# Loading two weight matrices with GpSimd's casting transfers, in a linear-attention and highway kernel

## The chip, the core and the metric

The kernel runs on one core of a Trainium2 chip. The metric is the device time of one execution in microseconds (us). Beside it stands a profile of one execution: its span runs from the first to the last instruction, and what the time has beyond the span lies around it. The engines are called PE (TensorE, matmuls and turning blocks), DVE (VectorE), ACT (ScalarE), POOL (GpSimd) and SP (SyncE, which here only issues transfers).

## The reference: what is computed

```python
q, k, v: (8, 8, 576, 64) fp32        # batch, heads, sequence, head size
q_s = softmax(q, axis=-1)            # over the 64 of a head
k_s = softmax(k, axis=2)             # over the sequence
kv  = einsum('bhsd,bhse->bhde', k_s, v)
att = einsum('bhsd,bhde->bhse', q_s, kv)
x   = att.transpose(0, 2, 1, 3).reshape(4608, 512)
H   = maximum(x @ w_h, 0)            # w_h, w_t: 512 x 512 fp32
T   = sigmoid(x @ w_t + b_t)
out = T * H + (1 - T) * x            # 4608 x 512 fp32
```

## The kernel before, in words

Every load, computation and store is a small function, and the string `ORDER` (lines 16 to 62) is a list of 683 steps, such as `mt_5_0`, that are issued one after the other. The order of the list is the order on each engine's queue and on each queue of transfers; an engine works through its own steps strictly in this order, and waits are put in where a step needs another's result or buffer. A letter behind a colon chooses the engine: `:A` is ACT, `:D` DVE, `:P` POOL, and `:F` takes a whole batch in one instruction. No planner runs when the kernel is built; the list is all there is.

The work is done batch by batch (8 batches) and in 36 tiles of 128 output rows. Nine tiles belong to two batches: four to each, and one that holds rows of both. The steps of a batch `b` are:

- `q_b_*`, `k_b_*`, `v_b_*`: loads, on SP's queue, of fp32 data. Batches 0 and 1 are loaded in pieces. A new transfer on SP waits until the eighth before it has landed, and until its buffer is free.
- `ek`, `eq`: exponentials on ACT, to fp16. `vc`: the cast of v to fp16 (POOL without a letter, or ACT, or DVE).
- `kv_b_*`: PE's products of exp(k) and v (72 small matmuls, or 36 for a half in batches 0 and 1). `kr`, `kn`: DVE divides by the sums and writes the small matrix `kvb`.
- `qt_b_g`: PE turns blocks of exp(q); `qc_b_g` copies them from PSUM to SBUF (DVE, or ACT with `:A`).

The steps of a tile `i` are:

- `xu_i`: PE multiplies turned q with `kvb`; `rs` and `x`: DVE divides by the row sums and writes x in fp16.
- `xt_i`: PE turns x into the PSUM tile `turned`; `xe_i` copies it out as `xT` (ACT, or DVE with `:D`).
- `bw_i`: the bias goes into the gate's PSUM tile, by a PE matmul or by a copy on ACT (`:A`). `mt_i`: PE multiplies `xT` with `w16["t"]`, four matmuls of 128x512. `mh_i`: the same with `w16["h"]`.
- `th_i`: tanh of half the gate on ACT. `dd_i`: DVE forms d = max(-x/2, ...) from x and the `mh` result. `uu_i`: (tanh + 1) times d, on DVE, or with `:P` as two instructions on POOL. `oo_i`: POOL adds x. `st_i`: the store, on SP's queue.

The weights are needed in fp16, and `w_h` in the form half of (w_h minus identity), so that one `max` and one product give the result. Before the change this takes four kinds of steps. `w_t_c` and `w_h_c` (line 208; c is 0 or 2, two blocks of 128 rows each) load fp32 weights, 512 KB a step, on SP's queue into a buffer of the pool for outputs (`o32`). `wtc_c` (line 217) casts w_t to fp16, here on POOL. `whd_c` (line 224) subtracts the identity from one 128x128 block in fp32, on POOL. `whc_c` (line 228) halves and casts w_h, on ACT.

Setup is part of the list as well. `setuppool` (line 148) lets POOL fill the tile `blank` with zeros and make two identity matrices; `setupdve` clears tiles on DVE. `fill_n` (line 165) issues n matmuls of `blank` that compute nothing that is used: they write into `turned`, and keep PE busy while it would wait. `bp` and `bc` spread the bias over all rows.

Of the kernel before, what the change touches and what calls it, by code (L numbers as in the profile page):

```python
# [22 lines left out]
xe_0_1 dd_3 xt_2_0 mh_0_1 mt_0_1 th_1_0 xe_2_0:D dd_0 vc_1_2:A kv_1_1 uu_1_0 oo_1_0 eq_1_0 mt_0_0 th_0_0 ek_1_0 ek_1_1
kr_1_1 bw_3 qt_1_0 vc_1_1:A kn_1_1 qc_1_0 mt_3_0 xu_5_1 uu_0_0 mh_2_0 th_3_0 bw_2 rs_5_1 x_5_1 dd_2 xu_4_1 kv_1_0
kr_1_0 eq_1_1 rs_4_1 xt_5_1 mt_2_0 th_2_0 kn_1_0 bw_5 xe_5_1:D x_4_1 xu_5_0 mt_5_1 qt_1_1 eq_1_2 rs_5_0 x_5_0 xt_5_0
xu_4_0 bw_4:A uu_3_0:P oo_3_0 xe_5_0:D mh_5_1 rs_4_0 x_4_0 mh_5_0 xt_4_1 qc_1_1:A xt_4_0 xe_4_1:D dd_5 eq_2_0 xe_4_0:D
v_4_0 mt_5_0 th_5_0 xu_6_0 qt_1_2 rs_6_0 qc_1_2 oo_0_0 mt_4_1 mh_4_1 mh_4_0 uu_2_0:P x_6_0 mt_4_0 eq_2_1 xt_6_0 xu_8_0
uu_5_0 bw_6:A xe_6_0:D qt_2_0 rs_8_0 x_8_0 mh_6_0 oo_5_0 th_4_0 xt_8_0 dd_4 uu_4_0 xu_7_0 mt_6_0 ek_2_0:F rs_7_0
vc_2_2:A bw_8 xe_8_0:D mt_8_0 x_7_0 th_6_0 xt_7_0 th_8_0 oo_2_0 vc_2_0 kv_2_0 oo_4_0 qc_2_0 q_4_0 bw_7:A qt_2_1
qc_2_1:A dd_6 uu_6_0:P oo_6_0 eq_3_0:F xe_7_0:D kr_2_0 kn_2_0 mh_8_0 xu_9_0 rs_9_0 x_9_0 mt_7_0 th_7_0 bw_9 dd_8  # L30
uu_8_0:P qt_2_2 qc_2_2:A xu_10_0 bw_10:A xt_9_0 xe_9_0:D rs_10_0 x_10_0 ek_3_0 mh_7_0 dd_7 ek_3_2 mh_9_0 xu_12_0 k_4_0
xt_10_0 k_5_0 rs_12_0 qt_3_0 xe_10_0:D x_12_0 mt_9_0 th_9_0 uu_7_0:P q_4_9 dd_9 xu_11_0 qc_3_0 vc_3_2:A xt_12_0
mt_10_0 rs_11_0 mh_10_0 x_11_0 v_5_0 q_5_0 vc_3_0 st_1_1 q_5_9 uu_9_0 dd_10 oo_7_0 kv_3_0 qt_3_1 th_10_0 oo_8_0 st_1_0
xe_12_0 bw_12:A mh_12_0 kr_3_0 qc_3_1:A kn_3_0 xu_14_0 rs_14_0 x_14_0 bw_11:A xt_11_0 xe_11_0 mt_12_0 th_12_0 qt_3_2
v_6_0 xt_14_0 oo_9_0 k_6_0 xu_13_0 q_6_0 xe_14_0 mh_11_0 dd_12 qc_3_2 mt_11_0 rs_13_0 eq_4_0:F th_11_0 uu_12_0
uu_10_0:P x_13_0 dd_11 xu_15_0 rs_15_0 vc_4_0 mh_14_0 x_15_0 st_5_1 dd_14 qt_4_0 oo_10_0 vc_4_2 xu_16_0 rs_16_0 x_16_0
xt_13_0 xe_13_0:D oo_12_0 bw_14:A bw_13:A ek_4_0:F st_3_0 mt_14_0 th_14_0 xu_17_0 rs_17_0 bw_15:A x_17_0 qc_4_0
xt_15_0 mt_13_0 kv_4_0 xe_15_0:D kr_4_0 uu_11_0:P oo_11_0 th_13_0 qt_4_1 uu_14_0:P st_3_1 mh_13_0 vc_5_2 xt_16_0
kn_4_0 mh_15_0 xe_16_0:D vc_5_0 xu_18_0 ek_5_0:F dd_13 xt_17_0 qc_4_1:A uu_13_0 xe_17_0:D dd_15 rs_18_0 oo_14_0
bw_16:A mt_15_0 mh_16_0 x_18_0 th_15_0 uu_15_0:P mt_16_0 dd_16 mh_17_0 oo_13_0 bw_17:A th_16_0 oo_15_0 kv_5_0 uu_16_0  # L40
kr_5_0 kn_5_0 oo_16_0 eq_4_2 dd_17 qt_4_2 xt_18_0 eq_5_0 mt_17_0 st_5_0 xe_18_0 xu_20_0 rs_20_0 mh_18_0 qc_4_2:A
bw_18:A q_7_0 th_17_0 mt_18_0 eq_5_1 bw_20:A uu_17_0:P x_20_0 xt_20_0 dd_18 vc_6_2 xe_20_0:D xu_21_0 th_18_0 rs_21_0
st_7_0 v_7_0 qt_5_1 qc_5_1:A mt_20_0 x_21_0 xt_21_0 uu_18_0 eq_5_2 xu_19_0 xe_21_0:D qt_5_0 rs_19_0 x_19_0 st_7_1
mh_20_0 qc_5_0 bw_21:A st_10_1 vc_6_0 mt_21_0 th_20_0 dd_20 ek_6_0:F xu_22_0 bw_19:A rs_22_0 x_22_0 qt_5_2 th_21_0
qc_5_2:A eq_6_0 mh_21_0 bw_22:A xt_19_0 xe_19_0:D kv_6_0 dd_21 kr_6_0 kn_6_0 xt_22_0 uu_20_0:P mh_19_0 mt_19_0
xe_22_0:D dd_19 oo_17_0 xu_23_0 rs_23_0 oo_20_0 oo_18_0 mt_22_0 eq_6_1 qt_6_0 th_19_0 x_23_0 xu_24_0 uu_19_0 th_22_0
xt_23_0 xe_23_0:D k_7_0 mh_22_0 rs_24_0 bw_23:A x_24_0 mt_23_0 qc_6_0 xu_25_0 rs_25_0 x_25_0 st_10_0 uu_21_0:P oo_19_0
xt_24_0 xe_24_0:D oo_21_0 mh_23_0 dd_22 uu_22_0:P xu_26_0 xt_25_0 oo_22_0 bw_24:A eq_7_0 mt_24_0 th_23_0 rs_26_0
x_26_0 qt_6_1 xe_25_0 vc_7_2 qd_7_0 xt_26_0 xu_27_0 vc_7_0 mh_24_0 dd_23 uu_23_0 rs_27_0 eq_7_1 q_7_9 qd_7_1 st_17_0
mh_25_0 x_27_0 qc_6_1:A bw_25:A xu_29_0 th_24_0 xe_26_0 dd_24 uu_24_0 mt_25_0 bw_26:A ek_7_0:F rs_29_0 x_29_0 th_25_0  # L50
oo_23_0 mh_26_0 dd_25 xt_27_0 xu_28_0 rs_28_0 xe_27_0:D x_28_0 mt_26_0 bw_27:A st_8_0 xt_29_0 xe_29_0:D eq_7_2 q_6_9
oo_24_0 mh_27_0 kv_7_0 dd_26 uu_25_0:P oo_25_0 th_26_0 xt_28_0 kr_7_0 mt_27_0 kn_7_0 mh_29_0 xe_28_0 dd_27 xu_31_0
st_14_1 bw_28:A mt_28_0 th_27_0 st_12_0 bw_29:A mt_29_0 dd_29 th_28_0 eq_6_2 rs_31_0 x_31_0 st_25_0 xu_30_0 xt_31_0
th_29_0 xe_31_0 qt_6_2 bw_31:A uu_26_0:P oo_26_0 rs_30_0 x_30_0 mh_28_0 st_12_1 uu_27_0:P st_21_0 st_14_0 qc_6_2:A
xt_30_0 xe_30_0 xu_33_0 st_16_1 oo_27_0 st_26_0 uu_29_0 oo_29_0 dd_28 st_19_0 uu_28_0:P rs_33_0 x_33_0 bw_30:A st_23_0
mh_31_0 dd_31 mt_31_0 xt_33_0 oo_28_0 xu_32_0 rs_32_0 xe_33_0:D th_31_0 mt_30_0 mh_30_0 x_32_0 qt_7_2 uu_31_0 xu_34_0
dd_30 mh_33_0 oo_31_0 bw_33:A rs_34_0 xt_32_0 x_34_0 th_30_0 xe_32_0:D qc_7_2:A uu_30_0 mt_33_0 st_28_0 st_31_0
mh_32_0 dd_33 th_33_0 uu_33_0 xu_35_0 bw_32:A rs_35_0 oo_33_0 xt_34_0 mt_32_0 bw_34:A xe_34_0:D mh_34_0 st_33_0 x_35_0
xt_35_0 mt_34_0 dd_32 th_32_0 bw_35_1 oo_30_0 st_16_0 st_30_0 uu_32_0 xe_35_0 oo_32_0 mh_35_0 th_34_0 bw_35_0 mt_35_0
th_35_0 mt_35_1 dd_34 uu_34_0 oo_34_0 dd_35 uu_35_0 st_32_0 th_35_1 uu_35_1 st_34_0 oo_35_0 st_35_0 oo_35_1:D  # L60
st_35_1:A
"""


# [1 line left out]
def kernel(  # L66
# [148 lines left out]


    def wt_cast(e, c):
        if e == "D":
            nc.vector.tensor_scalar_mul(w16["t"][:, c:c + 2], T[f"wt{c}"], 1.0)
        else:  # L220
            copy = nc.gpsimd.tensor_copy if e == "P" else nc.scalar.copy
            copy(w16["t"][:, c:c + 2], T[f"wt{c}"])

    def wh_less_identity(e, c):
        block = T[f"wh{c // 2 * 2}"][:, c % 2, c // 2 * 2 * P + c % 2:c // 2 * 2 * P + 2 * P:2]
        (nc.gpsimd if e == "P" else nc.vector).tensor_sub(block, block, idf)
# [307 lines left out]
```

## Time and profile before

| what | value |
|---|---|
| median of 3 runs | 118.77 us (118.72 to 118.85) |
| the profiled execution: its own time | 118.69 us |
| its span | 116.9 us |
| mean granted PE clock | 0.995 |
| bytes moved | 40.58 MB, of which 30.41 MB read from and 9.44 MB written to HBM |

A row of the timeline has the start and the busy time in us, the engine, the line of the code, the operation, its output and input, a count, and in brackets how long the engine sat idle before it and what ended that wait. PE's matmuls overlap, so the time of a row is longer than the distance from one to the next. Issuing a transfer is not counted as busy time.

### The profile page before, as it was taken

Reading aid. Unit: us, or ns where it says so; the run is one execution under the profiler, and the core shown is the slowest. Engines: PE = TensorE matmul, PEld = TensorE weight load, DVE = VectorE, ACT = ScalarE, POOL = GpSimd, SP = SyncE. Lnnn points to the kernel's source line nnn. Section 1 sums busy time; section 2 is a strip of 40 time slices with the busy share of each in tenths; the row PEclk is TensorE's granted clock in tenths of the full one; section 3 lists DMA queues with packets and bytes.
Section 4 is the critical chain, followed back from the end, with each engine's and each line's share of the span. In section 5 each row is a group of like instructions: output and inputs, shape, how many; then the busy total and the mean of one; then the engine's idle time right before and its main releaser. Section 6 shows DMA issues by size and latency. Waiting matters only on the chain.

```text
span 116.9 us, 3424 instructions
## 1 busy us (share of the span) xinstructions
PE 109.5 (94%) x1351; PEld 61.6 (53%) x1351; DVE 93.3 (80%) x222; ACT 90.0 (77%) x132; POOL 89.1 (76%) x99
## 2 busy tenths in 40 slices
...
GB/s 42 399 392 377 408 398 385 375 377 379 393 391 397 383 391 393 358 375 387 357 376 360 387 392 363 390 381 383 399 398 217 302 204 270 397 404 115 315 295 179
DMA packets 24195, 40.58 MB, mean 347 GB/s; under 512 B 5362, under 2 KB 11762, under 8 KB 24180
## 3 DMA queue, kind: packets, MB, share of 16 engines
...
q10 hardware_dynamic: 148, 0.14, 0.4%
...
HBM read 30.41 MB, written 9.44 MB: 341 GB/s over the span
## 4 chain that ended last, share of the span: by engine, by line
PE 67%; POOL 15%; issue 6%; DVE 5%; DMA 3%; SPq 1%; POOLq 0%; DVEq 0%
PE tps L411 18%; PE gps L419 16%; PE turned L167 9%; POOL o L471 7%; PE xu L361 6%; PE turned L384 5%; PE kv L269 5%; PE qps L324 4%; POOL u L451 4%; DMA out_dram<-o 3%; POOL g L450 2%; PE qps L319 2%; POOL v L259 2%; DVE x L376 2%; PE tps L401 1%
## 5 line engine op out<-in xcount | busy, mean ns | idle before, releaser
L471 POOL TENSOR_TENSOR o<-u,x 128x512 f32<-128x512 f16 (+1 forms) x36 | 40.6, 1143 | 1.6 <-DVE u L453 0.7
L411 PE MATMUL tps<-w16t,xT 128*128 128x512 f16 (+1 forms) x148 | 37.3, 373 | 0.0
L419 PE MATMUL gps<-w16h,xT 128*128 128x512 f16 x144 | 36.8, 379 | 0.5 <-DVE xT L391 0.5
L376 DVE TENSOR_TENSOR x<-xu,rs 128x512 f16<-128x512 f32 (+1 forms) x39 | 25.2, 649 | 2.4
L259 POOL CAST v<-v 128x1152 f16<-128x1152 f32 (+1 forms) x14 | 14.0, 1010 | 14.7 <-DMA v<-in_v_dram 13.7
L439 DVE SCALAR_TENSOR_TENSOR d<-x,gps 128x512 f16<-128x512 f16 x36 | 24.5, 680 | 0.3
L451 POOL TENSOR_TENSOR u<-g,d 128x512 f16<-128x512 f16 x17 | 19.7, 1158 | 1.7 <-DVE rs L370 0.4
L253 ACT ACTIVATE ek<-k 128x576 f16<-128x576 f32 (+2 forms) x15 | 17.9, 1225 | 3.0 <-DMA k<-in_k_dram 3.0
L419 PEld LDWEIGHTS <-xT 128*128 128x128 f16 x144 | 13.0, 98 | 12.3 <-DVE xT L391 1.8
L399 ACT COPY tps<-ball 128x512 f32<-128x512 f32 x28 | 16.6, 597 | 3.5 <-DVE u L453 3.2
L411 PEld LDWEIGHTS <-xT 128*128 128x128 f16 x148 | 13.2, 98 | 10.6 <-DVE xT L391 0.4
L361 PE MATMUL xu<-kvb,eq 128*128 128x130 f16 (+1 forms) x160 | 14.8, 224 | 0.2 <-DVE kvb L287 0.2
L384 PE MATMUL turned<-idh,x 128*128 128x128 f16 x144 | 14.2, 220 | 0.5 <-DVE x L376 0.5
L391 DVE COPY xT<-turned 128x512 f16<-128x512 f16 (+1 forms) x28 | 10.9, 391 | 4.2 <-PE turned L384 3.0
L435 ACT ACTIVATE tps<-tps 128x512 f32<-128x512 f32 (+1 forms) x20 | 11.2, 559 | 3.6 <-PE tps L411 3.3
L453 DVE SCALAR_TENSOR_TENSOR u<-tps,d 128x512 f16<-128x512 f32 (+1 forms) x19 | 12.7, 671 | 1.4 <-ACT tps L435 0.6
L361 PEld LDWEIGHTS <-eq 128*128 128x128 f16 (+1 forms) x160 | 10.0, 100 | 7.3 <-DVE x L376 2.5
L167 PE MATMUL turned<-blank 128*128 128x512 f16 x40 | 12.4, 458 | 1.5 <-POOL blank L149 1.3
L384 PEld LDWEIGHTS <-x 128*128 128x128 f16 x144 | 9.8, 98 | 6.0 <-DVE x L376 2.1
L307 ACT ACTIVATE qe<-q 128x1024 f16<-128x1024 f32 (+3 forms) x9 | 9.4, 1052 | 4.1 <-DMA q<-in_q_dram 4.1
L450 POOL TENSOR_SCALAR g<-th 128x512 f16<-128x512 f16 x17 | 10.6, 621 | 0.9 <-ACT th L433 0.9
L433 ACT ACTIVATE th<-tps 128x512 f16<-128x512 f32 x17 | 10.0, 594 | 0.9 <-PE tps L411 0.9
...
## 6 DMA issues: line engine op xcount, KB each, us to landing
...
v<-in_v_dram SPq DMA_DIRECT2D x6, 1152.0 KB, 12.0
...
```

Source lines behind the costliest of these rows:

```text
L167: nc.tensor.matmul(spare, blank[:, 0:P], blank, start=True, stop=True, skip_group_check=True)
L253: nc.scalar.activation(t[:, :, c:c + n].rearrange("p j c d -> p c j d"), T[f"k32{b}"][:, c:c + n].rearrange("p c (j d) -> p c j d", j=NJ), ...
L259: copy(v16[b % NV][:, c:c + n, :, 0:D], T[f"v32{b}"][:, c:c + n].rearrange("p c (j d) -> p c j d", j=NJ))
L361: nc.tensor.matmul(dst, turned_q(b, jp, n), kvb[b % NKV][:, hh, kk], start=True, stop=True, skip_group_check=True)
L376: nc.vector.tensor_mul(t[:, k0:k1], sums(i, k)[:, :, :, 0:64], T[f"rs{i}_{k}"][:, 0:k1 - k0].unsqueeze(3).to_broadcast([P, k1 - k0, 4, D]))
L384: nc.tensor.matmul(t[:, n], T[f"x{i}"][:, n0 + n % 2:n0 + 2 * P:2], idh, is_transpose=True, start=True, stop=True, skip_group_check=True)
L399: nc.scalar.copy(t[:, cs], ball[:, cs])
L411: nc.tensor.matmul(T[gate(i, k)][:, cs], T[f"xT{i}"][:, n], w16["t"][:, n, cs], start=False, stop=(n == parts[-1] and not first), skip_gro ...
L419: nc.tensor.matmul(t, T[f"xT{i}"][:, n], w16["h"][:, n], start=(first and n == parts[0]), stop=(n == parts[-1] and not (first and len(part ...
L439: nc.vector.scalar_tensor_tensor(t, T[f"x{i}"], -0.5, T[f"gps{i}"], op0=ALU.mult, op1=ALU.max)
L451: nc.gpsimd.tensor_mul(t, g, T[f"d{i}"])
L471: eng.tensor_add(t[:, cs], T[f"u{i}_{h}"][:, cs], T[f"x{i}"][:, cs])
```

## The change

The two weight matrices are loaded by POOL's queue instead of SP's. Such a transfer writes fp16 straight into `w16`, while it reads fp32 from HBM. The cast of w_t is then an empty step. The identity is subtracted and the half applied in place, in fp16. The weights no longer pass through the output buffers.

```diff
     def load_w(e, w, c):
         src = dict(t=moe_w_t, h=moe_w_h)[w]
-        T[f"w{w}{c}"] = op.tile([P, 2, DM], FP32, tag="o32", name=f"w32{w}_{c}")
-        nc.sync.dma_start(T[f"w{w}{c}"], src.rearrange("(c p r) n -> c p r n", p=P, r=2)[c // 2])
+        nc.gpsimd.dma_start(w16[w][:, c:c + 2], src.rearrange("(c p r) n -> c p r n", p=P, r=2)[c // 2])
...
     def wt_cast(e, c):
-        if e == "D":
-            nc.vector.tensor_scalar_mul(w16["t"][:, c:c + 2], T[f"wt{c}"], 1.0)
-        else:
-            copy = nc.gpsimd.tensor_copy if e == "P" else nc.scalar.copy
-            copy(w16["t"][:, c:c + 2], T[f"wt{c}"])
+        return
 
     def wh_less_identity(e, c):
-        block = T[f"wh{c // 2 * 2}"][:, c % 2, c // 2 * 2 * P + c % 2:c // 2 * 2 * P + 2 * P:2]
-        (nc.gpsimd if e == "P" else nc.vector).tensor_sub(block, block, idf)
+        block = w16["h"][:, c, c // 2 * 2 * P + c % 2:c // 2 * 2 * P + 2 * P:2]
+        (nc.gpsimd if e == "P" else nc.vector).tensor_sub(block, block, idh)
 
     def wh_cast(e, c):
         if e == "D":
-            nc.vector.tensor_scalar_mul(w16["h"][:, c:c + 2], T[f"wh{c}"], 0.5)
-        else:
-            nc.scalar.mul(w16["h"][:, c:c + 2], T[f"wh{c}"], 0.5)
+            nc.vector.tensor_scalar_mul(w16["h"][:, c:c + 2], w16["h"][:, c:c + 2], 0.5)
+        else:
+            nc.scalar.mul(w16["h"][:, c:c + 2], w16["h"][:, c:c + 2], 0.5)
```

The whole list of steps is also new. Its beginning, before and after:

```diff
-b_0 q_0_0 v_0_1 setupdve k_0_0 b_32 eq_0_0 bsplit setuppool fill_5 fill_8 bp v_0_0 bc qt_0_0 ek_0_1 v_0_3 ek_0_0 k_0_2
-v_0_2 vc_0_3:A bw_1 vc_0_0 ek_0_2 vc_0_2 q_0_4 vc_0_1:D ek_0_3 bw_0 w_h_0 fill_8 qc_0_0 whd_1:P kv_0_0 eq_0_1 w_h_2
-w_t_2 kr_0_0 whd_0:P whd_2:P w_t_0 k_1_2 v_1_2 q_1_0 k_1_0 v_1_0 fill_5 q_1_4 kn_0_0 q_2_0 k_2_0 eq_0_2 xu_0_0 v_2_0
-q_3_0 rs_0_0 whc_0:A x_0_0 k_3_0 fill_4 v_3_0 kv_0_1 fill_3 kr_0_1 kn_0_1 xu_0_1 rs_0_1 xu_1_0 rs_1_0 qt_0_1 x_1_0
-fill_6 whd_3:P qc_0_1 xt_1_0 xu_3_0 qt_0_2 qc_0_2:A xe_1_0:D fill_1 rs_3_0 x_3_0 x_0_1 xt_3_0 xu_2_0 rs_2_0 x_2_0
-wtc_2:P whc_2:A mh_1_0 wtc_0:P vc_1_3 ek_1_3 ek_1_2 vc_1_0 xe_3_0:D mh_3_0 dd_1 xt_0_1 xt_0_0 mt_1_0 xe_0_0:D mh_0_0
+w_t_2 setupdve setuppool fill_8 q_0_0 v_0_2 k_0_0 fill_6 b_32 b_0 bsplit bp eq_0_0 bc qt_0_0 ek_0_0 fill_8 k_0_2
+ek_0_3 bw_3 v_0_1 v_0_0 wtc_0 v_0_3 vc_0_2:D vc_0_3:D bw_1 fill_3 ek_0_1 q_0_4 qc_0_0 w_h_0 vc_0_1 fill_8 w_t_0
+vc_0_0:A kv_0_0 ek_0_2 kv_0_1 w_h_2 whd_2:P k_1_2 kr_0_0 fill_8 eq_0_1 qt_0_1 kr_0_1 v_1_2 eq_0_2 kn_0_0 kn_0_1 xu_1_0
+xu_0_0 q_1_0 whd_0 rs_1_0 x_1_0 xu_0_1 fill_5 qc_0_1:A rs_0_0 xu_3_0 x_0_0 rs_3_0 x_3_0 xt_1_0 xe_1_0 fill_5 ek_1_2
+whd_3 whd_1:P xt_3_0 mt_1_0 xe_3_0:D xt_0_0 rs_0_1 whc_2:D xu_2_0 xe_0_0 k_1_0 x_0_1 v_1_0 whc_0:D vc_1_3 rs_2_0 x_2_0
+q_1_4 qt_0_2 mt_3_0 qc_0_2 th_3_0 vc_1_2 th_1_0 mh_3_0 xt_0_1 xe_0_1:D dd_3 ek_1_3 uu_3_0:P mh_1_0 dd_1 eq_1_0 q_2_0
...
```

Both lists hold the same tiles and batches. What the rest of the list changes is the order and the engine of some steps:

| steps | before | after |
|---|---|---|
| `whd` on POOL / DVE | 4 / 0 | 2 / 2 |
| `whc` on ACT / DVE | 2 / 0 | 0 / 2 |
| `vc` on POOL / ACT / DVE | 14 / 5 / 1 | 11 / 7 / 2 |
| `uu` on DVE / POOL | 20 / 17 | 16 / 21 |
| `qc` on DVE / ACT | 10 / 12 | 15 / 7 |
| `xe` on DVE / ACT | 28 / 11 | 23 / 16 |
| `bw` on PE / ACT | 9 / 28 | 11 / 26 |
| matmuls of `fill` | 40 | 51 |

More of the change, by code (lines that the diff above doesn't have):

```diff
@@ L22 @@
-wtc_2:P whc_2:A mh_1_0 wtc_0:P vc_1_3 ek_1_3 ek_1_2 vc_1_0 xe_3_0:D mh_3_0 dd_1 xt_0_1 xt_0_0 mt_1_0 xe_0_0:D mh_0_0
[L23 to L61, printed above, removed]
+w_t_2 setupdve setuppool fill_8 q_0_0 v_0_2 k_0_0 fill_6 b_32 b_0 bsplit bp eq_0_0 bc qt_0_0 ek_0_0 fill_8 k_0_2
@@ new lines @@
+xt_2_0 kv_1_1 bw_0 xe_2_0 oo_3_0 kr_1_1 ek_1_1 mt_0_1 mh_0_0 kn_1_1 uu_1_0 mh_0_1 dd_0 qt_1_0 qc_1_0 mh_2_0 dd_2
+ek_1_0 vc_1_1 vc_1_0:A mt_0_0 th_0_0 xu_5_1 rs_5_1 x_5_1 kv_1_0 xu_4_1 eq_1_1 bw_2 oo_1_0 kr_1_0 mt_2_0 uu_0_0:P bw_5
+rs_4_1 xt_5_1 xe_5_1 kn_1_0 k_2_0 eq_1_2 xu_5_0 v_2_0 oo_0_0 x_4_1 xu_4_0 th_2_0 qt_1_1 q_3_0 mt_5_1 k_3_0 rs_5_0
+x_5_0 xt_5_0 qc_1_1 mh_5_1 xu_6_0 v_3_0 qt_1_2 uu_2_0:P bw_4 xe_5_0 mh_5_0 rs_4_0 x_4_0 rs_6_0 qc_1_2 xt_4_0 x_6_0
+xt_4_1 q_4_0 oo_2_0 eq_2_0 eq_2_1 mt_5_0 xe_4_0:D xu_8_0 q_5_9 xe_4_1:D dd_5 th_5_0 xt_6_0 mt_4_1 mt_4_0 mh_4_1 rs_8_0
@@ new lines @@
+x_8_0 uu_5_0:P oo_5_0 qt_2_0 qc_2_0 xe_6_0 mh_6_0 xu_7_0 rs_7_0 x_7_0 vc_2_0 qt_2_1 qc_2_1 ek_2_0:F bw_6 mt_6_0 mh_4_0
+dd_4 xt_8_0 th_4_0 uu_4_0:P oo_4_0 v_4_0 vc_2_2:A th_6_0 dd_6 uu_6_0:P xe_8_0 qt_2_2 eq_3_0:F k_4_0 oo_6_0 bw_7 kv_2_0
+kr_2_0 bw_8 mt_8_0 xt_7_0 kn_2_0 st_3_0 xu_9_0 th_8_0 mh_8_0 xe_7_0:D rs_9_0 x_9_0 mt_7_0 th_7_0 dd_8 xu_10_0 xt_9_0
+rs_10_0 qc_2_2:A bw_9:A xe_9_0:D x_10_0 k_5_0 mh_7_0 dd_7 qt_3_0 xu_12_0 xt_10_0 xe_10_0:D mh_9_0 ek_3_0:F mt_9_0
+rs_12_0 uu_7_0:P x_12_0 vc_3_2:A xu_11_0 th_9_0 uu_8_0 xt_12_0 rs_11_0 bw_10:A qc_3_0:A bw_12:A x_11_0 eq_4_0
@@ new lines @@
+xe_12_0:D dd_9 mh_10_0 vc_3_0 kv_3_0 kr_3_0 oo_8_0 v_5_0 xt_11_0 mt_10_0 kn_3_0 xe_11_0 qt_3_1 oo_7_0 dd_10 xu_14_0
+qc_3_1 rs_14_0 mt_12_0 th_10_0 x_14_0 uu_10_0 mh_12_0 xu_13_0 rs_13_0 x_13_0 xt_14_0 xe_14_0:D q_4_9 eq_4_1 q_5_0
+mh_11_0 uu_9_0:P qt_3_2 bw_11:A th_12_0 qc_3_2 xu_15_0 mt_11_0 vc_4_2:A bw_14:A rs_15_0 oo_9_0 x_15_0 th_11_0 vc_4_0
+dd_12 qt_4_0 oo_10_0 xu_16_0 rs_16_0 x_16_0 xt_13_0 xe_13_0:D qc_4_0 mt_14_0 st_3_1 uu_12_0:P oo_12_0 xu_17_0 bw_13:A
+rs_17_0 ek_4_0:F th_14_0 xt_15_0 xe_15_0:D bw_16:A mt_13_0 mh_14_0 qt_4_1 v_6_0 dd_11 uu_11_0:P oo_11_0 x_17_0 kv_4_0
@@ new lines @@
+xt_16_0 dd_14 mh_13_0 qc_4_1 xe_16_0:D mh_16_0 kr_4_0 wtc_2 th_13_0 st_1_0 bw_15:A xt_17_0 kn_4_0 mt_16_0 ek_5_0
+ek_5_2 xe_17_0:D dd_13 uu_14_0:P oo_14_0 vc_5_0 dd_16 uu_13_0:P th_16_0 oo_13_0 k_6_0 xu_18_0 uu_16_0 oo_16_0 rs_18_0
+x_18_0 eq_4_2 vc_5_2:A mt_15_0 st_1_1 mh_15_0 th_15_0 mh_17_0 qt_4_2 xt_18_0 dd_15 uu_15_0 kv_5_0 oo_15_0 bw_17:A
+xe_18_0:D q_6_0 mt_17_0 eq_5_0 bw_18:A mt_18_0 kr_5_0 kn_5_0 qc_4_2 xu_20_0 eq_5_1 qt_5_1 dd_17 th_17_0 rs_20_0 x_20_0
+mh_18_0 xt_20_0 uu_17_0 xu_21_0 st_5_0 st_5_1 vc_6_0 xe_20_0:D th_18_0 rs_21_0 x_21_0 qc_5_1:A qt_5_0 mh_20_0 bw_20:A
@@ new lines @@
+vc_6_2 st_7_1 dd_18 xt_21_0 xe_21_0:D xu_19_0 rs_19_0 x_19_0 q_7_0 k_7_0 dd_20 bw_21:A mt_20_0 mt_21_0 qc_5_0:A st_7_0
+xu_22_0 ek_6_0:F th_21_0 uu_18_0:P oo_18_0 rs_22_0 x_22_0 eq_5_2 xt_19_0 xe_19_0:D mh_21_0 st_10_0 kv_6_0 mh_19_0
+th_20_0 v_7_0 xt_22_0 kr_6_0 kn_6_0 qt_5_2 bw_22:A oo_17_0 bw_19:A qc_5_2:A uu_20_0:P xu_23_0 rs_23_0 oo_20_0 mt_19_0
+xe_22_0:D x_23_0 dd_21 eq_6_0:F q_6_9 mt_22_0 th_22_0 dd_19 xt_23_0 th_19_0 xe_23_0:D xu_24_0 rs_24_0 x_24_0 bw_23:A
+mh_22_0 mh_23_0 uu_21_0:P eq_7_0:F uu_19_0 xt_24_0 bw_24:A xu_25_0 rs_25_0 mt_23_0 x_25_0 qt_6_0 qc_6_0:A xe_24_0:D
```

13 lines of the change are left out of this document (added).

## The prediction, on record before the result was known

> **What bounds the kernel now.** I read the page's busy line first, then the windows by stage, then the chain of waits at the start, then the timelines of GpSimd, ScalarE and the queues over the first 20 us.
>
> ```profile
> PE 109.5 (94%) x1351; PEld 61.6 (53%) x1351; DVE 93.3 (80%) x222; ACT 90.0 (77%) x132; POOL 89.1 (76%) x99
> ```
> ```profile
> 1.31:19.67 18.36, 17.06 (x163) 8.19 (x163) 11.03 (x38) 9.65 (x13) 5.62 (x12) 1.00 1.01 367
> 19.67:38.90 19.23, 19.23 (x218) 10.40 (x221) 15.96 (x42) 17.01 (x24) 12.14 (x14) 1.00 1.06 384
> 38.90:92.80 53.90, 53.88 (x773) 32.12 (x773) 48.11 (x106) 50.05 (x70) 51.46 (x52) 1.00 1.08 370
> 92.80:112.10 19.30, 19.29 (x207) 10.88 (x206) 16.52 (x34) 12.88 (x26) 17.76 (x18) 1.00 0.76 289
> ```
>
> Columns: window, length, then busy time of PE, PEld, DVE, ACT, POOL, the granted clock, the DMA share and GB/s. From 19.67 to 112.10 PE shows no idle time. Busy PE is not yet useful PE, so I priced each PE step of the list at the start-to-start times of the chain: 0.86 us for the four matmuls of an mt or mh, 0.23 for an xu, 0.22 for an xt or a bias matmul (bw without a letter), 0.45 for eight turned q blocks, 0.37 or 0.74 for a kv. From mh_3 on that makes 89.4 us of work in 92.4 us. PE therefore is the bound over 92 us, with 3.0 us of waits inside: 18.0 us of steps fill the first 19.23, so 1.2 of the 3.0 lies there. After PE's end come 4.8 us (last tanh, gate, add and store) to the span's end, and 1.8 between the span, 116.9, and this execution's 118.69. GpSimd is the second bound: busy 51.46 of 53.90 us in the middle. DMA is full (share above 1) until about 90 us.
>
> What stands before 19.67 decides when PE's block can begin:
>
> ```profile
> 0.73 0.54 POOL blank L149
> 1.31 5.59 PE turned L167 x13
> ...
> 8.21 1.73 PE turned L167 x8
> 9.94 0.41 PE kv L269 x34
> ...
> 17.68 0.40 PE turned L384 x4
> ...
> 19.67 1.04 PE gps L419 x4
> 20.70 0.22 PE turned L384 x4
> 20.93 0.86 PE tps L411 x4
> ```
>
> GpSimd fills the tile blank, which releases the dummy matmuls (L167): 0.43 us each for the first 13, 0.216 after. They stand in PE's queue in program order, so each also delays what is listed behind it.
>
> ```profile
> 7.74 0.66 POOL L259 CAST v<-v 128x576 f16<-128x576 f32 x1 [5.46 <-DMA v<-in_v_dram]
> ...
> 15.13 0.89 POOL L226 TENSOR_TENSOR w32h<-w32h,idf 128x128 f32<-128x128 f32 x2 [0.38 <-DMA w32h<-in_moe_w_h_dram]
> ...
> 19.01 1.04 POOL L222 CAST w16t<-w32t 128x1024 f16<-128x1024 f32 x1 [0.27 <-DMA w32t<-in_moe_w_t_dram]
> ```
> ```profile
> 4.68 1.06 ACT L307 ACTIVATE qe<-q 128x1024 f16<-128x1024 f32 x1 [1.83 <-DMA q<-in_q_dram]
> ...
> 12.52 1.36 ACT L307 ACTIVATE qe<-q 128x1024 f16<-128x1024 f32 x2 [1.29 <-DMA q<-in_q_dram]
> ```
>
> Each of these started as its load landed. In the order of SP's queue 1664 KB were in at 7.74, 3456 at 12.52 and 4480 at 15.13: 381 KB per us. Weights come behind all of batch 0, whose work thus hides their transfer.
>
> **What is removed.** Two weight casts on GpSimd (2 x 1.04) and two halvings on ScalarE (2 x 1.06), 4.2 us. I cost their removal at nothing by itself: before 22 us GpSimd waits for loads (5.46, 2.35, 2.44 us before three of its steps) and ScalarE is busy 9.65 of 18.36. They did set the weights' readiness: the second halving ended at 18.03 and mh_1 began at 18.14. What is late next is x: the xT of tile 3 ends at 19.6, and mh_3 waits for it. So at most 1.5 us could have come from here. Four issues on SP (0.98 for two) also go; SP is far ahead there.
>
> **What is added.** (a) Four transfers on GpSimd's queue; w_t_2 stands ahead of blank. No row shows a GpSimd transfer. The nearest are SP's issue of the same weights, 0.49 each, and ScalarE's, 0.40; I take 0.49 and bound it by 0 and by 2.3 us (a start-up hold, below). The Trainium skill, DMA: Bandwidth & Descriptors, "Specifications", gives about 1 us to the first byte on this path; that would put blank 0.5 later and the sum up to 0.5 higher.
>
> (b) The halving on DVE, 128x1024 in fp16, twice. Nearest rows: DVE's copy of 128x1024 fp16 from PSUM, 0.68, and that of 128x512, 0.41; I take 0.55, bounds 0.3 and 0.68. Subtracting the identity in fp16: at most the 0.46 of the fp32 row.
>
> (c) Bytes. SP's first loads in the new list are q_0_0 512 KB, v_0_2 288, k_0_0 and k_0_2 576 each, v_0_1, v_0_0, v_0_3 288 each, q_0_4 640. w_t_2 and w_h_0, 1024 KB, are now issued in the first 4 us and share the DMA engines with them. If they are done before v_0_1, each landing is SP's own sum plus 1024: v_0_1 3264 KB, 12.0 us; v_0_0 3552, 12.8; v_0_3 3840, 13.5; q_0_4 4480, 15.1.
>
> **Walk of the new start.** PE: blank 0.49 late gives 1.80; 13 cold fills 5.59; 20 warm ones 4.3; bp 0.44, qt_0_0 0.45, two bias matmuls 0.43: kv_0_0 could start at 13.0. It needs v_0_0 cast on ScalarE: 12.8 + 0.66 = 13.4. kv_0_1 needs v_0_3 cast on DVE: 13.5 + 0.75 = 14.3, ends 14.7; fill_8 1.73 to 16.4; eq_0_1 is ready (15.1 + 1.06), qt_0_1 to 16.9; three xu steps 0.46, fill_5 1.08, xu_3 0.23, xt_1 0.22: 18.9. The next fill_5 writes the tile turned, which ScalarE must first copy out (0.59; a row of the waits shows a fill waiting for xT today): 19.5, fills to 20.6, xt_3, and mt_1 starts at 20.8 instead of the 19.67 at which the old block became solid: +1.13.
>
> By then PE has done less. Both lists have by that point qt_0_0, qt_0_1, two bw, kv_0, xu_0, xu_1, xu_3, xt_1, xt_3. The old one has also mh_1 0.86, xu_2 0.23, qt_0_2 0.11; the new has two more bias matmuls in all, 0.43: +1.63.
>
> mh_3: w_t_0 and w_h_2 are queued behind GpSimd's cast of v_0_1 (12.0 to 12.7), issued by 13.7. The first q, 512 KB, took 3.95 us from issue to use, 2.6 beyond its bytes; so their bytes start at about 15.8 and at half the rate take 5.4: 21.2. DVE's whd_3 waits for this, and behind it in DVE's queue stand xe_3, both halvings and x_0_1: whc_0 ends near 23.7 where PE would reach mh_3 at 23.0. Between 0 and 0.7; I take 0.35.
>
> Credit: of the 1.2 us of waits in 19.67 to 38.90, part are for batch 1, whose loads have the same bytes ahead of them as before while PE comes later. Between 0 and 1.2; I take 0.6.
>
> Sum: 1.13 + 1.63 + 0.35 - 0.6 = +2.5 on PE's end. The tail's 4.8 us and the 1.8 outside the span stay. 118.69 + 2.5 = **121.2 us**; the median of the runs, 118.77, is 0.08 above the profiled execution, so either base gives the same.
>
> **Edits of the list in the middle.** uu on GpSimd goes from 17 to 21 tiles (0.62 + 1.16 each there, 0.69 on DVE), v casts on GpSimd from 14 to 11, DVE's copies of turned q from 10 to 15 (0.68; 1.01 on ScalarE), xT copies from DVE to ScalarE, 5. Summed from the rows, GpSimd has 83.7 us from oo_1 on instead of 82.9, DVE 0.9 less. SP's store issues keep their number; nine stores precede the last large load in both lists, so the last loads land alike.
>
> **Rivals.** *GpSimd bounds:* uu_3 at about 24.7 puts oo_1 at 28.4 (27.19 today); 0.8 more work and today's 3.3 of gaps: +2.0, 120.7. For: 95% busy in the middle; against: PE's +2.5 covers it. *Descriptor hold:* GpSimd's first transfer stalls while DVE clears its tiles (0.82 to 3.6), which delays blank by 2.3 instead of 0.49; kv_0_0 is then PE-bound at 14.8 instead of 13.4: +1.4, 122.6. Against: GpSimd's own memsets run beside DVE's today. The Trainium skill, SBUF — State Buffer, "Who interferes with whom", has DVE's two-port copies lock GpSimd out of writing descriptors; no row here shows it. *Faster:* PE's 3.0 us of hidden waits shrink below what the start costs. Place: 19.67 to 112.10. If the new transfers take little from SP's, mt_1 is held by program order alone at 19.8 and the start costs 0.1 + 1.63 = 1.7; beyond 1.7 of waits saved it is faster. With 2.8 saved: 117.6. For: 4.2 us of ScalarE and GpSimd work gone, DVE 0.9 lighter; against: it lies where those engines idle. *No effect:* weights no longer decide anything and the rest cancels: 118.7.
>
> **How the numbers follow.** Forecast 0.50, GpSimd 0.09, hold 0.18, faster 0.17, no effect 0.06. The bounds give 0.1 + 1.63 - 1.2 = +0.5 (119.2) at the low end and 1.13 + 1.63 + 0.7 + 1.4 = +4.9 (123.6) at the high end. Reaching to part of the faster case: 118.0 to 123.2. A measurement here tells about 0.2% from no change. Faster 0.18, same 0.06, slower 0.76.
>
> **What would show it.** PE's first dummy matmul at 1.7 to 2.4; kv_0 after 13 us; the first L406 (mt) row near 20.8, PE solid to about 114.6, and the chain's start running through v loads. Wrong if kv_0 starts by 11, if mt_1 starts by 19, if mh_3 waits for the halvings beyond 24, or if PE's block is shorter than 92 us.

## The result, and the profile after

The changed kernel takes **121.93 us** (median of 4 runs, 121.77 to 122.03) against 118.79 (118.72 to 118.85) for the kernel before: a ratio of 1.0263, interval 1.0245 to 1.0280. The profiled execution took 121.77 us, its span is 120.0. The forecast was 121.2.

The views are read in the same order as before. First the busy line of the page:

```profile
PE 110.2 (92%) x1364; PEld 63.6 (53%) x1364; DVE 93.0 (77%) x223; ACT 89.5 (75%) x129; POOL 92.5 (77%) x104
```

PE has 0.7 us more work by this count (thirteen more matmuls, eleven of them dummies) while the span grew by 3.1. So most of the loss is idle time or time filled with dummies, and it has to be found in a stage. The windows of the changed kernel, cut where the first mt and the first mh start (window, length, then busy time of PE, PEld, DVE, ACT, POOL, granted clock, DMA share, GB/s):

```profile
2.59:20.54 17.95, 16.67 (x163) 8.59 (x164) 8.31 (x26) 8.62 (x13) 3.00 (x8) 1.00 1.06 335
20.54:23.72 3.18, 2.51 (x20) 1.30 (x18) 2.16 (x7) 0.37 (x1) 2.04 (x4) 1.00 1.06 401
23.72:40.00 16.28, 16.28 (x200) 9.61 (x199) 13.91 (x37) 14.42 (x21) 14.21 (x16) 1.00 1.06 387
40.00:93.00 53.00, 52.79 (x764) 31.86 (x763) 47.30 (x106) 48.94 (x65) 50.11 (x51) 1.00 1.07 361
93.00:115.30 22.30, 21.92 (x225) 12.21 (x223) 19.08 (x40) 16.10 (x31) 20.66 (x21) 1.00 0.68 261
```

PE is solid from 23.72, where before it was from 19.67; between 20.54 and 23.72 it does 2.2 us of steps in 3.2. In the middle PE (52.79 of 53.00) is still ahead of GpSimd (50.11). What set the start stands in the chain of waits of the first 26 us:

```profile
2.77 8.68 DMA v<-in_v_dram
11.45 0.06 issue
11.51 0.66 POOL v L254
12.17 0.47 POOL w16t L209
12.64 8.89 DMA w16h<-in_moe_w_h_dram
...
21.56 0.03 DVE w16h L220
21.60 0.17 issue
21.77 0.43 DVE xT L386
22.20 0.04 issue
22.24 0.27 PE turned L379 x2
...
22.86 0.86 PE tps L406 x4
23.72 0.96 PE gps L414 x4
```

Two transfers fill it: v_0_1, the first v that GpSimd casts in the new list, in at 11.51, and w_h_2, which GpSimd can issue only behind the cast of that v, and which takes 8.89 us. (In the old list GpSimd casts v_0_0 first, in at 7.74; here v_0_0 is in at 12.23.) GpSimd's timeline shows the new transfers (start, length, instruction, and in brackets the idle time before it and what ended it):

```profile
1.24 0.75 POOL L209 DMA_DIRECT2D w16t<-in_moe_w_t_dram  x1 [0.80 <-POOLq L513]
1.99 0.54 POOL L148 MEMSET blank<- 128x512 f16 x1
...
3.51 0.56 POOL L209 DMA_DIRECT2D w16h<-in_moe_w_h_dram  x1
11.51 0.66 POOL L254 CAST v<-v 128x576 f16<-128x576 f32 x1 [7.44 <-DMA v<-in_v_dram]
12.12 0.53 POOL L209 DMA_DIRECT2D w16t<-in_moe_w_t_dram  x1
12.64 0.54 POOL L209 DMA_DIRECT2D w16h<-in_moe_w_h_dram  x1
21.68 0.85 POOL L220 TENSOR_TENSOR w16h<-w16h,idh 128x128 f16<-128x128 f16 x2 [8.50 <-DMA w16h<-in_moe_w_h_dram]
```

ScalarE's first large step on the second half of q comes later for the same reason (12.52 before):

```profile
14.79 1.36 ACT L302 ACTIVATE qe<-q 128x1024 f16<-128x1024 f32 x2 [1.30 <-DMA q<-in_q_dram]
```

The queue lines of the page (packets, MB, share of 16 engines' span) show what the casting transfers cost:

```profile
q1 hardware_dynamic: 23456, 38.15, 90.2%
q0 software_dynamic: 576, 1.05, 4.6%
```

The profile counts the fp16 bytes written, 1.05 MB, but they occupied 4.6% of 120.0 = 5.5 us. SP's queue, which no longer carries the 2.1 MB of fp32 weights, went from 96.9% of 116.9 = 113.3 us to 90.2% of 120.0 = 108.2, 5.1 less. So no time on the DMA engines was saved.

### The profile page after: what moved, and what is told of

It is laid out like the page before. It is cut to its first block, busy times and chain, and to the rows that moved or that the text cites. A ratio compares the mean times of both kernels' runs of the same rounds, so it can differ in the third digit from the quotient of the medians.

```text
span 120.0 us, 3461 instructions
## 1 busy us (share of the span) xinstructions
PE 110.2 (92%) x1364; PEld 63.6 (53%) x1364; DVE 93.0 (77%) x223; ACT 89.5 (75%) x129; POOL 92.5 (77%) x104
## 3 DMA queue, kind: packets, MB, share of 16 engines
q1 hardware_dynamic: 23456, 38.15, 90.2%
q0 software_dynamic: 576, 1.05, 4.6%
## 4 chain that ended last, share of the span: by engine, by line
PE 70%; DMA 15%; POOL 5%; issue 3%; SPq 2%; DVE 1%; POOLq 1%
PE gps L414 23%; PE tps L406 22%; DMA w16h<-in_moe_w_h_dram 7%; DMA v<-in_v_dram 7%; PE xu L356 7%; PE turned L379 7%; PE kv L264 4%; PE qps L319 3%; POOL o L466 3%; PE qps L314 2%; PE tps L396 1%; SPq L182 1%; POOL u L446 1%; POOLq L524 1%; DVE u L448 1%
## 5 line engine op out<-in xcount | busy, mean ns | idle before, releaser
L406 PE MATMUL tps<-w16t,xT 128*128 128x512 f16 (+1 forms) x148 | 36.8, 373 | 0.0
L446 POOL TENSOR_TENSOR u<-g,d 128x512 f16<-128x512 f16 x21 | 24.3, 1158 | 3.4 <-DVE d L434 1.1
L406 PEld LDWEIGHTS <-xT 128*128 128x128 f16 x148 | 13.5, 98 | 10.9 <-DVE xT L386 0.2
L394 ACT COPY tps<-ball 128x512 f32<-128x512 f32 x26 | 15.2, 594 | 2.6 <-DVE u L448 2.4
L254 POOL CAST v<-v 128x1152 f16<-128x1152 f32 (+1 forms) x11 | 11.0, 1006 | 7.4 <-DMA v<-in_v_dram 7.4
L166 PE MATMUL turned<-blank 128*128 128x512 f16 x51 | 13.3, 410 | 3.3 <-POOL blank L148 2.6
L428 ACT ACTIVATE th<-tps 128x512 f16<-128x512 f32 x21 | 12.5, 595 | 4.0 <-PE tps L406 4.0
L445 POOL TENSOR_SCALAR g<-th 128x512 f16<-128x512 f16 x21 | 13.0, 620 | 0.8 <-ACT th L428 0.8
L386 ACT COPY xT<-turned 128x512 f16<-128x512 f16 (+1 forms) x16 | 8.7, 547 | 6.2 <-PE turned L379 6.1
L430 ACT ACTIVATE tps<-tps 128x512 f32<-128x512 f32 (+1 forms) x16 | 9.0, 561 | 2.8 <-PE tps L406 2.7
L448 DVE SCALAR_TENSOR_TENSOR u<-tps,d 128x512 f16<-128x512 f32 (+1 forms) x15 | 10.0, 669 | 1.2 <-POOL o L466 0.6
```

The costliest lines, as they stand in the source:

```text
L166: nc.tensor.matmul(spare, blank[:, 0:P], blank, start=True, stop=True, skip_group_check=True)
L394: nc.scalar.copy(t[:, cs], ball[:, cs])
L406: nc.tensor.matmul(T[gate(i, k)][:, cs], T[f"xT{i}"][:, n], w16["t"][:, n, cs], start=False, stop=(n == parts[-1] and not first), skip_gro ...
L445: nc.gpsimd.tensor_scalar(g, T[f"th{i}"], 1.0, 1.0, op0=ALU.add, op1=ALU.mult)
L446: nc.gpsimd.tensor_mul(t, g, T[f"d{i}"])
```

## The experiments

All kernels are the changed one with an edit, unless said. Theory: the loss is made before 24 us, by weights whose bytes stand ahead of batch 0 and by others that come late; after that PE's list is worked off with 2 to 3 us of waits whatever was done. The rivals are a bound by GpSimd, the late blank, and the extra transfers by themselves. The ratio stands with its interval; what PE does in the tables is from its timelines.

**E1: the new list, with the old loads and casts.** The old functions in the new list; SP's queue carries fp32 weights in the new places.

```diff
-... v_0_0 wtc_0 v_0_3 ...  w_h_2 whd_2:P ... whc_2:D ... whc_0:D ... kr_4_0 wtc_2 th_13_0
+... v_0_0 v_0_3 ... w_h_2 wtc_2:P wtc_0:P whd_2:P ... whc_2:A ... whc_0:A ... kr_4_0 th_13_0
```

> The new list with the old loads: fp32 weights on SP's queue at the new list's places, cast on GpSimd and halved on ScalarE. By the theory that the start decides (PE's solid block begins late, because of the order and the dummy matmuls at the head of the new list and because of the late landing of w_h_2), half of the loss is the list's: SP's sums put v_0_0 at 11.4 us, mt_1 near 19.4 and mh_3 near 22.5 instead of 23.7, so 120.4 to 121.2 us. If the transfers on GpSimd's queue alone cost the time: 118.8. If the middle of the new list (more uu on GpSimd) costs it: 121.9.

Measured 121.32 us, ratio 1.0191 (1.0144 to 1.0238), 0.1 us above what the theory gave and below the 121.9 of its second rival. No transfer of GpSimd is in it, and most of the loss is there. v_0_1 is in at 10.97, since the weights stand early in SP's queue too; mt_1 runs at 20.03, and PE waits for the second halving:

```profile
20.03 1.03 PE L410 MATMUL tps<-w16t,xT 128*128 128x512 f16 x4
...
23.42 1.02 PE L418 MATMUL gps<-w16h,xT 128*128 128x512 f16 x4 [1.04 <-ACT w16h L231]
```

So the list, with its place for the weights, costs about 1.9% by itself. That leaves some 0.7% for what GpSimd's transfers add here; the two intervals are only just apart.

**E2: the old list with GpSimd's transfers.** The kernel before with the new functions, the four transfers together behind GpSimd's first cast.

```diff
-... bw_1 vc_0_0 ek_0_2 ... bw_0 w_h_0 fill_8 ... eq_0_1 w_h_2 w_t_2 kr_0_0 ... w_t_0 k_1_2
+... bw_1 vc_0_0 w_h_0 w_h_2 w_t_2 w_t_0 ek_0_2 ... bw_0 fill_8 ... eq_0_1 kr_0_0 ... k_1_2
```

> The old list with the new transfers, all four queued on GpSimd behind the cast vc_0_0 (about 8.4 us). By the theory that the start decides, the weights' 2 MB now take half of the DMA engines while q_0_4 and v_0_2 are loading: q_0_4 near 15.5 instead of 12.5, mh_1 near 20.3 instead of 18.1: 120.3 to 121.5 us. If the new list alone is to blame: 118.8 or less (ScalarE and GpSimd have 4 us less to do).

Measured 122.23 us, ratio 1.0288 (1.0224 to 1.0351): worse than expected. The transfers were issued from 8.67 to 11.0, yet w_h_0 was in only at 15.76 and w_h_2 at 18.80, so PE waited and its clock then fell:

```profile
17.93 0.59 PE L415 MATMUL gps<-w16h,xT 128*128 128x512 f16 x2
20.75 1.63 PE L415 MATMUL gps<-w16h,xT 128*128 128x512 f16 x6 [2.23 <-ACT w16h L227]
22.17 0.63 PE L380 MATMUL turned<-idh,x 128*128 128x128 f16 x4
22.60 1.91 PE L407 MATMUL tps<-w16t,xT 128*128 128x512 f16 x4
```

The four matmuls at 22.60 took 1.91 where they take 1.03 elsewhere. One half of the change loses 1.9%, the other, in these places, 2.9%, and the whole 2.6%: their losses don't add.

**E3: blank ahead of the first transfer.**

```diff
-w_t_2 setupdve setuppool fill_8
+setupdve setuppool w_t_2 fill_8
```

> The new kernel with w_t_2 queued behind the setup on GpSimd, so that blank is filled as early as in the old kernel (PE's first matmul near 1.3 instead of 2.6 us). By the theory of the late loads nothing is won, since kv_0 at 12.95 waited for v_0_0 and not for PE: 121.5 to 122.2 us. If the late blank is what makes the start late: 1.3 us less, 120.6.

Measured 122.89 us, ratio 1.0304 (1.0237 to 1.0371), above the 121.5 to 122.2 that was expected; its interval overlaps that of the changed kernel. The dummies begin at 1.32 instead of 2.59, and the kernel is not faster for it: PE runs out of dummies before the loads are in (v_0_0 at 12.70, 0.5 later than in the changed kernel).

```profile
9.33 2.54 PE L166 MATMUL turned<-blank 128*128 128x512 f16 x11
13.43 1.48 PE L264 MATMUL kv<-v,ek 64*64 64x65 f16 x72 [1.56 <-ACT v L254]
14.84 3.35 PE L166 MATMUL turned<-blank 128*128 128x512 f16 x8
```

Eight dummies take 3.35 us instead of the 1.90 of the changed kernel: half the clock, after a pause of 1.56 us. So an earlier blank gains nothing here; the late one kept the dummies beside the loads.

**E4: four uu back from GpSimd.** The uu of tiles 4, 6, 20 and 23 go to DVE, those of 20 and 23 ahead of the bw that reuses their PSUM tile.

```diff
-uu_4_0:P ... uu_6_0:P ... bw_22:A ... uu_20_0:P ... bw_26:A uu_23_0:P
+uu_4_0 ... uu_6_0 ... uu_20_0 bw_22:A ... uu_23_0 bw_26:A
```

> The new kernel with four of the 21 uu steps (4, 6, 20, 23) taken from GpSimd to DVE, two of them a few places earlier in the list: GpSimd 17 as before, 7.1 us less for it, 2.7 more for DVE. By the theory that PE's start decides, 121.5 to 122.3 us. If GpSimd is the bound in the new kernel: 1.5 to 3 us less, near 119.5.

Measured 126.11 us, ratio 1.0592 (1.0547 to 1.0638), outside what either theory gave. GpSimd has 7 us less to do and the kernel is 4 us slower. Its longest waits between 30 and 110 us, then the same three in the changed kernel (total, times, longest):

```profile
POOL g L445 <- ACT th L428: 5.7, 3, 3.0
POOL o L466 <- DVE u L448: 5.2, 4, 2.0
ACT tps L394 <- DVE u L448: 5.2, 4, 2.1
```
```profile
POOL g L445 <- ACT th L428: 0.5, 2, 0.3
POOL o L466 <- DVE u L448: 0.2, 1, 0.2
ACT tps L394 <- DVE u L448: 1.6, 3, 1.0
```

A uu on DVE reads the gate's PSUM tile, so ScalarE's next bias copy waits for it. Work was therefore not the limit there, the order of the waits was. The run shows that less work on GpSimd does not by itself make the kernel faster. As the edit also moved waits, it does not measure what GpSimd's work costs, and it says nothing of what 17 uu would cost in a list made for them.

**E5: w_h first.** w_h_2 and w_h_0 take the two early places, w_t the late ones, which need no halving; DVE subtracts and halves ahead of vc_0_3; mh comes ahead of mt for tiles 1 and 3. **E6** is E5 without the five dummies between xt_1 and xt_3.

```diff
-w_t_2 ... w_h_0 vc_0_1 fill_8 w_t_0 ... w_h_2 ... mt_1_0 ... mt_3_0 ... mh_3_0 ... mh_1_0
+w_h_2 setupdve setuppool w_h_0 ... whd_2 whd_3 whc_2:D whd_0 whd_1 whc_0:D vc_0_3:D ... vc_0_1 fill_8 w_t_0 ...
+w_t_2 ... mh_1_0 ... mh_3_0 ... mt_3_0 ... mt_1_0
```

> The new kernel with the transfers of w_h ahead of those of w_t; the identity and the half are applied by DVE while it waits for v_0_3 (7 to 13 us, idle in the new kernel), and the mh of tiles 1 and 3 stand ahead of their mt. So nothing waits for the last weight at 21.5 us. By the rule that PE's end is the start of its solid block plus the list's remaining work plus the 2.35 us of waits that the new list showed in three kernels: start 20.5 with 91.1 left, PE's end 114.0 instead of 114.9, 120.6 to 121.2 us where the new kernel has 121.9. If the late w_h_2 cost nothing: unchanged.

> As e5_h_first, and the five dummy matmuls behind xe_1 left out. In the new kernel they wait for ScalarE's copy of xT_1 and then take 1.08 us. By the rule the block begins when x_3 is there (19.3) and turned, at 19.6, one us before e5: PE's end 113.0, 119.6 to 120.2 us. If dummy matmuls only fill what PE would wait for anyway: as e5.

E5: 121.32 us, ratio 1.0203 (1.0180 to 1.0225). E6: 120.62 us, ratio 1.0144 (1.0120 to 1.0167). Both gained, but less than expected: they are 0.1 and 0.4 us above the ranges given, with starts 0.5 and 0.3 later than reckoned. The wait for w_h is gone; PE's block begins with mh_1, in E6 at 19.87:

```profile
19.63 0.40 PE L379 MATMUL turned<-idh,x 128*128 128x128 f16 x4 [0.80 <-DVE x L371]
19.87 1.03 PE L414 MATMUL gps<-w16h,xT 128*128 128x512 f16 x4
```

By the ratios, taking away the hold by w_h_2 gives back 0.7 of the changed kernel's 3.1 us, and dropping five dummies 0.7 more. E6 is the fastest kernel found with these transfers, and it still loses 1.4%: at 19.87 it has more of its list before it than the old kernel had at 19.67 (91.1 against 89.4 us, priced as in the prediction).

**E7: an earlier block in the kernel before.** xe_3 is moved ahead of rs_2 on DVE.

```diff
-... xu_2_0 rs_2_0 x_2_0 ... vc_1_0 xe_3_0:D mh_3_0
+... xu_2_0 xe_3_0:D rs_2_0 x_2_0 ... vc_1_0 mh_3_0
```

> The old kernel with one step moved: xe_3 (DVE's copy of xT_3) stands ahead of rs_2 and x_2 in DVE's queue, so mh_3 need not wait for x_2 (18.59 to 19.28). By the rule the block becomes solid at about 19.0 instead of 19.67: 0.4 to 0.7 us less, 118.1 to 118.4. If the start does not set the end (GpSimd or the loads do): 118.8, unchanged.

Measured 118.97 us, ratio 1.0008 (0.9989 to 1.0028): unchanged, a miss. mh_1 and mh_3 now run as one from 18.37, but kv_1_1 starts at 23.29 (23.24 before): xt_2 waits 0.33 us for an xT of ScalarE, which itself had waited for a k of batch 1 until about 20.5. An earlier start counts only until the next load; the changed kernel is late enough for its start to count in full (E6 begins its block 1.14 us ahead of E5 and ends it 1.27 ahead).

**E8: the changed kernel without five dummies** (those between xt_1 and xt_3).

```diff
-xt_1_0 xe_1_0 fill_5 ek_1_2
+xt_1_0 xe_1_0 ek_1_2
```

> The new kernel with only the five dummy matmuls behind xe_1 left out, w_h_2 still late. mt_1 comes near 19.6, but xe_3 stands behind whd_3, which waits for w_h_2 at 21.5, so mt_3 starts at 22.7 as before: 121.7 to 122.1 us, or up to 1.7 more if PE's clock falls in the longer idle stretch, as it did in e3_blank_first. If the dummy matmuls alone delay the start: 120.9.

Measured 122.07 us, ratio 1.0292 (1.0242 to 1.0342), a time as expected, though mt_1 came at 20.36 and not near 19.6. Without the dummies PE is simply at the next wait earlier:

```profile
20.36 1.02 PE L406 MATMUL tps<-w16t,xT 128*128 128x512 f16 x4 [0.21 <-DMA w16t<-in_moe_w_t_dram]
22.48 0.27 PE L379 MATMUL turned<-idh,x 128*128 128x128 f16 x2 [1.10 <-DVE xT L386]
```

The same edit that gained 0.7 us in E6 gains nothing here, so the late w_h_2 holds PE at 22.5 to 23.9 however the block begins.

**E9: all four transfers behind the cast of v_0_1. E10:** E9 without the five dummies.

```diff
-w_t_2 setupdve ... qc_0_0 w_h_0 vc_0_1 fill_8 w_t_0 ... kv_0_1 w_h_2 whd_2:P
+setupdve ... qc_0_0 vc_0_1 w_t_2 w_t_0 w_h_0 w_h_2 fill_8 ... kv_0_1 whd_2:P
```

> The changed kernel with all four casting transfers behind GpSimd's cast of v_0_1 (w_t_2, w_t_0, w_h_0, w_h_2 in this order), nothing else changed. Theory, that the two early transfers' bytes delay batch 0: v_0_1 is in at 9.2 to 9.6 instead of 11.5, v_0_3 at about 11.0 instead of 13.0, and the first product of k and v starts at about 12.5, when the fills ahead of it are through, not when a load lands. mt_1 then starts at 19.4 to 20.0 instead of 20.5. All 2 MB of weights now come in 10 to 22, so w_h_2 is in at 21.5 to 22.5 and mh_3 still waits for the halving, to 23.4 to 24.2. Time 121.3 to 122.2: little is won, because the late weights hold what the early loads give. Rival, that the place of these bytes does not matter: v_0_1 still at about 11.5 and the time 121.9.

> The same, and without the five dummy matmuls between the turning of tiles 1 and 3. Theory: mt_1 up to 1.0 us earlier than with them if w_t_0 is in by then (18.5 to 19.2), but mh_3 still waits for w_h_2 and its halving on DVE (23.4 to 24.2), so the time stays within 0.3 of the kernel with the fills, 121.2 to 122.2. Rival, that the start of the block decides and the late w_h_2 does not: 120.3 to 120.9.

E9: 128.00 us, ratio 1.0746 (1.0693 to 1.0800). E10: 125.92 us, ratio 1.0596 (1.0542 to 1.0650). The theory of the bytes holds where it was tested: v_0_1 is in at 9.38 and kv_0 starts at 12.07 without a wait. The time is far outside both expectations. DVE's timeline of E9 has the cause, one line that was overlooked:

```profile
13.15 1.20 DVE L282 TENSOR_TENSOR kvb<-kv,rz 64x128 f16<-64x128 f32 x4
21.29 0.30 DVE L220 TENSOR_TENSOR w16h<-w16h,idh 128x128 f16<-128x128 f16 x1 [6.94 <-DMA w16h<-in_moe_w_h_dram]
21.62 0.21 DVE L365 RECIPROCAL rs<-xu 128x8 f32<-128x8 f32 x1
```

whd_0 stands ahead of rs_1 in DVE's queue. With w_h_0 late it waits 6.94 us, and the row sums that PE needs wait behind it; PE idles 6.0 us and goes on at half the clock (0.55 granted from 22.7 to 29.0). E10 is 2.1 us faster because its five dummies, 2.29 us at that clock, are gone.

**E11: E9 with DVE's subtractions and halvings put together behind x_0_1.**

```diff
-q_1_0 whd_0 rs_1_0 ... ek_1_2 whd_3 whd_1:P ... rs_0_1 whc_2:D xu_2_0 ... x_0_1 v_1_0 whc_0:D
+q_1_0 rs_1_0 ... ek_1_2 whd_1:P ... rs_0_1 xu_2_0 ... x_0_1 v_1_0 whd_0 whd_3 whc_2:D whc_0:D
```

> The list of e9 (all four casting transfers behind GpSimd's cast of v_0_1), and DVE's two identity subtractions and two halvings taken out from among the first tiles' steps and put together behind x_0_1. Theory: the 6.0 us that PE idled in e9 were one DVE step, whd_0, that waited for w_h_0 and held the row sums of tile 1 behind it. Without it the row sums follow xu_1 at about 15.6, PE is through its five fills by 16.7 and reaches mt_1 at 18.6 to 19.6; mh_3 then waits for w_h_2 (in at about 22.9 as in e9) and the two halvings, until 24.3 to 25.0. That is 0.6 to 1.3 later than in the changed kernel: 122.4 to 123.4, or up to 1.5 more if PE's wait ahead of mh_3 halves its clock. Rival, that late weights hold PE by mt_1 as well: mt_1 at 22 or later and 125 or more.

Measured 124.77 us, ratio 1.0457 (1.0381 to 1.0533), in the range left for a fall of the clock. PE, by its timeline:

```profile
19.43 1.02 PE L406 MATMUL tps<-w16t,xT 128*128 128x512 f16 x4 [0.28 <-DMA w16t<-in_moe_w_t_dram]
...
20.75 1.03 PE L406 MATMUL tps<-w16t,xT 128*128 128x512 f16 x4
24.95 1.02 PE L414 MATMUL gps<-w16h,xT 128*128 128x512 f16 x4 [3.18 <-DVE w16h L224]
25.81 0.28 PE L379 MATMUL turned<-idh,x 128*128 128x128 f16 x2
25.92 1.82 PE L414 MATMUL gps<-w16h,xT 128*128 128x512 f16 x4
```

mt_1 is 1.1 us earlier than in the changed kernel and mh_3 1.2 later. That is the exchange in one picture: whichever of batch 0 and the weights has its bytes first, the other is late, and the old order (batch 0, weights, batch 1, in one queue) let PE's block begin at 19.67 with less left to do.

## Why the prediction was right, point by point

**The sum** was +2.5 us on PE's end; PE's last matmul ended at 112.09 before and at 114.92 after, +2.83. The tail, taken as unchanged, is 0.26 longer. PE's last rows, before and after:

```profile
111.05 1.04 PE L411 MATMUL tps<-w16t,xT 128*128 128x256 f16 x8
```
```profile
113.88 1.04 PE L406 MATMUL tps<-w16t,xT 128*128 128x256 f16 x8
```

Term by term:

| step | predicted | measured |
|---|---|---|
| mt_1 against the old block's start | +1.13 (20.8) | +0.87 (20.54) |
| work left by then | +1.63 | +1.63 (priced, not timed) |
| hold ahead of mh_3 | +0.35 (0 to 0.7) | +1.0 (3.18 us for 2.17 of steps) |
| waits later in PE's block | -0.6 (0 to -1.2) | -0.7 (2.3 left of 3.0) |
| tail after PE's end | 0 | +0.26 |

The mechanism was as forecast. That the sum is only 0.3 short is in part luck: the walk to mt_1 was reckoned 0.26 too long and the hold 0.65 too short.

**What failed in size** is the hold ahead of mh_3. The end of the halvings was reckoned well: near 23.7, and whc_0 ended at 23.61, although w_h_2 landed at 21.54 and not 21.2. But the prediction took only half of the distance from PE's arrival (23.0) to that end, and PE was 0.3 earlier still. So w_h_2 and the steps that wait behind it set the start of mh_3: the chain of waits above runs from v_0_1 over w_h_2 to mh_3 and not through mt_1, and the first and third rows of the table are not independent. The first effect of w_h_2 was also one step ahead: xe_3, behind whd_3 on DVE, held the turning of x at 22.24 (0.67 us) before the halvings held mh_3. E8 shows this hold, E5 its absence.

**After mh_3** the new list takes the same time wherever it begins. From the start of mh_3 to PE's end the timelines have 91.2 to 91.4 us in the changed kernel, E1, E3, E8, E9 and E10, though mh_3 starts anywhere from 23.4 (E1) to 29.8 (E9). Only E4 (95.4) and E11 (92.9, with part of it at half the clock) need more. The old list takes 92.4 from its mh_3. So neither the middle of the new list nor the loads after 24 us made the loss; it lies ahead of mh_3, 4.0 us, of which the shorter rest gives 1.2 back.

**Landings.** v_0_1, v_0_0, v_0_3 and q_0_4 were in at 11.51, 12.23, 13.00 and 14.79, each 0.3 to 0.6 earlier than 12.0, 12.8, 13.5 and 15.1. The rule that the early 1024 KB are counted ahead of batch 0 was therefore right to 0.6 us; E9 shows the other side of it, 9.38 with none of them ahead.

**blank** was 1.28 us late, not 0.49: GpSimd's first instruction of the list began at 1.24 instead of 0.73, and the issue took 0.75. The first dummy came at 2.59, outside the 1.7 to 2.4 named as a sign. In the profiled execution it mattered nothing, as kv_0 waited 0.45 us for a load (see also E3). It was close, though: the first 14 dummies took 4.50 us there and 5.75 in the profiled execution of E4, whose list begins the same; in E4 kv_0 began without a wait at 13.69 instead of 12.95, and mt_1 at 20.75 instead of 20.54.

**Costs on DVE.** The two halvings took 0.62 and 0.54 (taken: 0.55; 0.40 and 0.41 each in E9), a subtraction 0.30 to 0.40 (taken: at most 0.46).

**Rivals.** *GpSimd bounds:* oo_1 came at 28.90 (28.4 forecast), but PE was busy 52.79 of 53.00 us in the middle, and all of PE's waits from mh_3 on come to 2.3 us, the most that relieving another engine could give. E4, with 7 us less on GpSimd, was slower. *Descriptor hold:* the first transfer ran from 1.24 to 1.99 in the midst of DVE's clearing, and took the same 0.75 us from 2.22 on in E3, still beside it. In E11, long after the clearing, the first two transfers took 1.30 together (0.75 and 0.56 here). No stall to 3.6 is seen. The rule of the Trainium skill, SBUF — State Buffer, "Who interferes with whom", that was named beside this rival, speaks of DVE's two-port copies; the run shows no lock by these memsets. A cast of v on DVE ran beside issues in E11 (10.77 to 11.52) and both took their usual time, but no run shows whether that cast is of the two-port kind, so the rule itself stays untested. *Faster:* 0.7 us of waits were saved where more than 1.7 were needed. *No effect* is excluded by the interval.

**The rest of the range** was wide enough for the result but not for its neighbours: a step at the wrong place of a queue costs 3.2 us (whd_0 in E9 against E11, where three more steps move with it) and four moved uu cost 4.2 (E4), which no rival here had priced.

**The tail.** From PE's end to the end of the profiled execution it is 6.60 us before, 6.61 in E7 and 6.52 in E1, which has the new list without GpSimd's transfers; it is 6.85 in the changed kernel, 6.96 in E2, which has the old list with them, and 6.82 to 6.90 in the others. So the 0.26 us go with the transfers and not with the order of the last steps. Of the 0.6 us between the profiled executions of E1 and the changed kernel, 0.33 are this tail.

What stays open: why GpSimd's queue starts 0.5 us later when a transfer is the first step; why the tail is longer with GpSimd's transfers; and how much these cost at the start apart from their place.
